# Two pieces of ScalarE work tied behind the kept product u3 in the second block of gates

## The chip, the cores and the metric

The kernel runs on one core of one Trainium2 chip. The metric is the device time of one execution in microseconds (us). A profiled execution gives the trace; other executions are timed without it.

## What is computed

For each of 8 batches and 8 heads of 64 features over 576 tokens:

```
kv  = k^T v                                (64 x 64 per head)
o   = q kv
x   = o / sqrt(mean(o*o) + 1e-6) * g_norm
```

The heads are laid side by side, so x is 4608 tokens by 512. Then

```
a = x w1;  b = x w2          (512 x 1024)
out = ((a * b) w3) w_out     (1024 x 1024, 1024 x 512)
```

q, k, v and g_norm are float32. The four weights arrive as float64 and are turned to float32 on the chip.

## The kernel before, in words

**Stages.** Weights come in chunks into four raw buffers. A chunk is *converted* from 64-bit words in steps (`conversion`, L137): ScalarE makes the low words (L158, into a part of `ab`) and the absolute value of the high words (L160, into the destination); VectorE then runs four passes (L162, L166, L169, L172); a chunk of w1 and w2 is scaled by g_norm at the end (L133 on ScalarE in the first group). There are 20 chunks. The first eight and some more are used at once, since w3 w_out is folded into one matrix `w3o_sb` at the start (`fold_chunk`, L681). The last four, chunks 2, 6, 3 and 7 of w1 and w2, are converted during the first group of gates. I call the last one w7.

**Groups.** The tokens are worked in nine groups of 512 (eight batches, and one of what is left of them). A group has four *blocks of gates* (p = 0 to 3) and then a projection. A block computes a part of a, b and a*b by Winograd's form of a two by two matrix product (`winograd`, L695): seven products on TensorE (L702), in three PSUM banks r1, r2, r3:

```
r1 = a11*b11, copied as p1;   r2 = s1*t1, copied as p5
r1 += s2*t2,  copied as u2;   (between)
r2 += s4*b22, c12;            r1 += s3*t3, copied as u3, c22
r3 = a12*b21, c11;            (between)
r1 += a22*t4, c21
```

The copies p1, p5, u2 and u3 are ScalarE's (`keep`, L713, copy at L715), each into a buffer of its name that exists once (u2 and u3 share one). A product that adds into a bank can't start before the copy of that bank has been taken. c11, c12 and c22 are VectorE's sums of a bank and a copy (L844) and a product (L845); c21 is a ScalarE copy (L839) and a VectorE product (L841).

**Work in the gaps.** At each `between` a piece of the attention of the next batch is issued (`steps`, L572; batch 1 during the first group). The first `between` of the second block (p = 1) issues the kv products of batch 1 (L334) and their six ScalarE copies (L342, L344). The second one issues `end_first`: q of batch 1, two tiles, was taken apart by ScalarE (L295), turned by a DMA transpose (L297), and is put together again by two ScalarE copies (L307). Behind each of them in SyncE's queue stands the load of the next q into the same tile (`load_q_ahead`, L472, at L95). The first `between` of the third block issues the product of q and kv (L412).

**What sets the order.** TensorE, GpSimd and SyncE run in the order of the program text (`manual_schedule`, L1288). ScalarE and VectorE are ordered by a planner when the kernel is built, from its own durations. `tc.issue_after(x)` ties the instructions in its block behind x where they are on x's engine. It adds no wait between engines. The conversions of the first group are begun at L1477 to L1484 after each block, two of them per block while there are some (n = 0, 1); the first two steps are tied behind a copy of that block, `ahead`. For p = 1 and n = 1 the chunk is w7; its VectorE passes and its scaling are issued at the first `between` of the third block (`between`, L1400). Its reader is the sum for the fourth block (`sum_w(3)`), issued after the third.

Of the kernel before, what the change touches and what calls it, by code (L numbers as in the profile page):

```python
# [22 lines left out]
def kernel(  # L23
# [64 lines left out]
    loaded, copies, adds = {}, {}, {}  # L88
# [164 lines left out]
    def all_of(steps):  # L253
        for _ in steps:
            pass
# [12 lines left out]
    xT = {B: x_left}  # L268
# [242 lines left out]
    def batch(b):  # L511
        if b not in batches:
            batches[b] = attention(b)
        return batches[b]
# [57 lines left out]
    def steps(b):  # L572

        a = batch(b)
        a.start()
        more = b + 1 < B
        fs, ends = ([[] for _ in range(8)] for _ in range(2))  # L580

        def turn(i, f, *args, next_group=False):

            t = []

            def begin():
                t.append(f(*args))
                next(t[0])
                next(t[0])

            fs[i].append((begin,))
            (to_end if next_group else ends[i + 1]).append((lambda: all_of(t[0]),))

        if to_end:

            ends[0] += [(lambda: nc.gpsimd.tensor_copy(tick, late["p5"][:, 0, 0:1]),), *to_end]
        to_end.clear()
        odd = b % 2
        by_scalar, in_two = b >= FIRST_OF_TWO, b > FIRST_OF_TWO
        if b == 1:  # L600
            early.extend(a.q_two_by_dma(r) for r in (0, 1))
            q_first = list(early)
            fs[0].append((a.begin_kv, 0))

            def end_first():
                for t in q_first:
                    with tc.issue_after(copies["kv"].ins):
                        next(t)
                    all_of(t)

            ends[1].append((end_first,))
        fs[2 if b == 1 else 1] += [(a.begin_kv, 1), (a.finish, 0)]
        if b == 1:
            last = {}

            def begin(name, behind, f, *args):
                last[name] = f(*args)
                with tc.issue_after(copies[behind][-1].ins):
                    next(last[name])
                next(last[name])  # L620

            def end(name, behind):
                with tc.issue_after(copies[behind][-1].ins):
                    next(last[name], None)
                all_of(last[name])

            fs[2] += [(begin, f"q{r}", "u2", a.q_two_by_dma, r) for r in (2, 3)]
            fs[3].append((begin, "left", "u3", a.q_left_by_dma))
            fs[4].append((begin, "x", "u3", a.x_by_dma, 0, nc.scalar.copy))
            ends[4] += [(end, "q2", "p1"), (end, "q3", "p5")]  # L630
            ends[5] += [(end, "x", "u2"), (end, "left", "u3")]
        elif by_scalar:
            turns_by_scalar(b)
        else:
            turn(1, a.q_two_by_dma, 2, 3)
            turn(2, a.x_by_dma, 0)
            if odd:
                turn(1, a.q_left_by_dma)
        second = 5 if b == 1 else 4
        if more:  # L640
            fs[6 if in_two else second].append((batch(b + 1).begin_kv, 0))
        fs[second].append((a.finish, 1))
        if odd:
            fs[3 if in_two else second + 1].append((a.product_left,))
        if b == 1:
            turn(6, a.x_by_dma, 1)
            turn(7, a.x_left_by_dma, next_group=True)
        else:
            if not by_scalar:
                turn(5, a.x_by_dma, 1)  # L650
            if odd:
                turn(5, a.x_left_by_dma, next_group=more)
        if more and not by_scalar:
            turn(7 if b == 1 else 5, batch(b + 1).q_two_by_dma, 0, 1, next_group=True)
        if more:
            fs[7 if odd else 0].append((load_q_left, b + 1))
        return iter([lambda s=e + f: [f(*args) for f, *args in s] for e, f in zip(ends, fs)])
# [101 lines left out]
    def run(*step_lists):  # L759

        for steps in zip(*step_lists):
            for step in steps:
                step()
# [52 lines left out]
    def sum_ab(p):  # L816
        aa[p] = {f"a{i + 1}{j + 1}": ab[j][:, p, i, :] for i in range(2) for j in range(2)}
        return sums(aa[p], free["ab", p])
# [300 lines left out]
    def sum_inner(n, between=lambda: None, place=None):  # L1119

        s1, s2, s4 = ab_sums
        x = [ab[0][:, :, 0], s1, s2, s4, ab[0][:, :, 1], ab[1][:, :, 0], ab[1][:, :, 1]][n]
        a11, a12, a21, a22 = (
            x[:, 2 * j:2 * j + 2, i * P:(i + 1) * P] for i in range(2) for j in range(2)
        )
        s1, s2, s4 = inner_sums[(n if place is None else place) % 3]
        nc.vector.tensor_add(s1, a21, a22)
        nc.vector.tensor_sub(s2, s1, a11)
        nc.vector.tensor_sub(s4, a12, s2)
        between()  # L1130
        nc.vector.tensor_sub(a21, a11, a21)
        inner[n] = [a11, a12, a22, s1, s2, s4, a21]
# [258 lines left out]
    for n, T in enumerate(groups):  # L1391
# [28 lines left out]
        if T in IN_TWO:  # L1420
            p = 2
# [15 lines left out]
        for p in range(NF):  # L1437
            if T in IN_TWO and p + 1 < NF:
                continue
            stage[0] = f"p{p}" if T in IN_TWO or T == FIRST_OF_TWO - 1 else None  # L1440
            if T and p + 1 == NF:
                sum_1, sum_2, sum_4, sum_3 = sum_ab(p)
                following = {
                    "c12": [], "c22": [sum_1],
                    "c11": [
                        lambda: sum_inner(0, lambda: all_of(f() for f in (sum_2, sum_3))),
                        lambda: sum_inner(1),
                    ],
                    "c21": [sum_4],
                }  # L1450

                if T in IN_TWO:
                    following["c22"].append(of_two[0])
                    following["c21"].append(of_two[1])
                if T not in TWICE:
                    in_order = tc.manual_schedule(engines={mybir.EngineType.DVE})
                    in_order.__enter__()
                gates(T, p, between, lambda name: all_of(f() for f in following[name]))
                continue
            gates(T, p, between if T or p else lambda: None)  # L1460
            if T == 0:

                def begin_early(behind):
                    t = early.pop(0)
                    with tc.issue_after(behind.ins):
                        next(t)
                    next(t)

                if p == 0:
                    begin_early(copies["xT"])  # L1470
                if p + 1 < NF:
                    ops = sum_w(p + 1)
                    if p != 2:
                        ops.pop(0)()
                    with tc.issue_after(adds["c12"][p].ins):
                        run(ops)
                for n in range(2):  # L1477
                    if len(converted) < len(todo):
                        ahead = [copies["p5"][p] if p else copies["xT"], copies["u2"][p]][n]
                        with tc.issue_after(ahead.ins):  # L1480
                            begin_next()
                        if len(begun) < len(todo):
                            with tc.issue_after(adds["c12"][0].ins):
                                end_next()  # L1484
                if p == 0:
                    begin_early(copies["u3"][0])
                if p + 1 == NF:
                    allocate_projection()
                    first, *others = zip(*(f(i) for i in range(NF) for f in (sum_ab, combine_w3o)))
                    with tc.issue_after(adds["c21"][p - 2].ins):  # L1490
                        all_of(step() for step in first)
                    with tc.issue_after(adds["c12"][p - 1].ins):
                        all_of(step() for steps in others for step in steps)
            else:
                ops = [step() for step in sum_ab(p)]
                with tc.issue_after(ops[-1].ins):
                    if p == 1:
                        prepare_some(3)
                    if (T, p) == (1, 1):
                        all_of(preparing)  # L1500
# [44 lines left out]
```

## Time and profile before

| | us |
|---|---|
| median of three runs | 751.8 |
| lowest and highest | 750.62, 752.29 |
| the profiled execution | 750.54 |
| its span in the trace | 748.7 |

In the trace's times, the first group's gates run from 84.1 us to about 140.7 and its projection to about 165. In the second block:

| ScalarE or TensorE work | start, us |
|---|---|
| p1, p5 | 97.96, 99.69 |
| u2 | 102.29 |
| low words of chunk 3 (L158) | 102.75 |
| absolute value of w7 (L160) | 103.83 |
| scaling of chunk 6 (L133) | 104.87 |
| kv copies | 105.91 to 107.23 |
| q copies (L307, two) | 107.13 to 109.36 |
| u3 | 109.38 |
| low words of w7 (L158) | 109.86 |
| TensorE, a22*t4 | 110.02 |
| c21 copy | 112.05 |
| p1 of the third block | 113.99 |

A time that a line gives as busy is from the first start to the last end of a run of equal instructions; neighbours on one engine overlap by about 0.1 us, so the spacing of starts is the cost of an instruction to its queue. "PE" is TensorE's matmuls, "PEld" its weight loads, "DVE" is VectorE, "ACT" ScalarE, "POOL" GpSimd, "SPq" SyncE's queue. The bracket at the end of a line holds the idle time of the engine before it, and what ended it.

### The profile page before, as it was taken

What the parts mean: (1) busy time and instruction counts of PE and PEld (TensorE: products, weight loads), DVE (VectorE), ACT (ScalarE), POOL (GpSimd) and SP (SyncE); (2) the same over time, 40 slices, a digit from 0 to 9 for tenths busy, and PEclk for the clock granted to TensorE, in tenths of its full rate; (3) what the DMA queues carried; (4) which work ended last, traced back from release to release, by engine and by line L of the source; (5) the groups of instructions that cost most, each with busy time, mean ns of one, the idle gap of its engine ahead of it and who ended that gap; (6) DMA issues with size and microseconds to landing.
All of it is one profiled execution on the core that took longest, in us unless ns stands there. A gap on an engine that the chain in (4) does not pass through costs nothing.

```text
span 748.7 us, 16771 instructions
## 1 busy us (share of the span) xinstructions
PE 740.2 (99%) x6759; PEld 659.3 (88%) x6759; DVE 640.2 (85%) x1339; ACT 361.3 (48%) x630; POOL 41.9 (6%) x46
## 2 busy tenths in 40 slices
PE   8999989999999999999999999999999999999998
PEld 6455778888899889999999999999999999999997
DVE  6977998747889877988898989898989997898897
ACT  6687777413321565347535763565367323222321
POOL 0000000133330100010000000100001000000000
PEclk9999999999999999999999999999999999999999
DMA  9996934438998996677967897689657663465354
GB/s 311 360 317 200 268 106 109 133 78 266 277 315 302 269 273 181 221 237 211 292 220 239 221 276 262 208 241 284 241 123 242 209 220 105 153 221 176 126 200 139
DMA packets 134737, 165.32 MB, mean 221 GB/s; under 512 B 77956, under 2 KB 110724, under 8 KB 134660
## 3 DMA queue, kind: packets, MB, share of 16 engines
q1 hardware_dynamic: 132208, 149.84, 66.0%
q10 hardware_dynamic: 2452, 14.42, 5.7%
q8 instruction: 53, 0.87, 0.5%
q14 instruction: 24, 0.20, 0.1%
HBM read 126.22 MB, written 20.71 MB: 196 GB/s over the span
## 4 chain that ended last, share of the span: by engine, by line
PE 95%; ACT 2%; DVE 1%; DMA 1%; issue 1%; SPq 0%; ACTq 0%
PE mm L702 42%; PE mm L1169 23%; PE mm L960 18%; PE mm L681 6%; PE at L334 2%; PE at L412 1%; PE mm L412 1%; PE at L668 1%; DMA raw<-in_moe_w_out_dram 1%; PE at L1220 0%; ACT ab L158 0%; DVE ab L162 0%; PE at L431 0%; ACT chunks L160 0%; ACT w_sb L160 0%
## 5 line engine op out<-in xcount | busy, mean ns | idle before, releaser
L702 PE MATMUL mm<-xT,w_sb 128*128 128x256 f32 x528 | 121.2, 380 | 0.0
L702 PEld LDWEIGHTS mm<-xT,w_sb 128*128 128x128 f32 x528 | 99.7, 191 | 13.3 <-issue 0.5
L702 PE MATMUL mm<-xc,ws 128*128 128x256 f32 x384 | 87.0, 380 | 0.0
L702 PEld LDWEIGHTS mm<-xc,ws 128*128 128x128 f32 x384 | 73.0, 190 | 10.1 <-ACT p L715 0.4
L681 PE MATMUL mm<-chunks,ab 128*128 128x512 f32 x128 | 60.4, 604 | 0.9 <-DVE chunks L172 0.9
L715 ACT COPY u<-mm 128x512 f32<-128x512 f32 x42 | 24.6, 585 | 59.8 <-PE mm L702 43.5
L715 ACT COPY p<-mm 128x512 f32<-128x512 f32 x50 | 29.4, 588 | 46.9 <-PE mm L702 30.6
L1180 ACT COPY u<-mm 128x512 f32<-128x512 f32 x23 | 13.5, 586 | 77.3 <-DVE raw L1193 39.8
L1169 PE MATMUL mm<-w3o_sb,ab 128*128 128x128 f32 x368 | 48.6, 276 | 0.0
L702 PE MATMUL mm<-xc,w_sb 128*128 128x256 f32 x192 | 46.4, 385 | 2.1 <-ACT u L715 2.1
L1169 PE MATMUL mm<-w3o_sb,raw 128*128 128x128 f32 x372 | 48.1, 276 | 0.0
L960 PE MATMUL mm<-ws,w3o_sb 128*128 128x128 f32 x300 | 46.3, 276 | 0.0
L1169 PEld LDWEIGHTS mm<-w3o_sb,ab 128*128 128x128 f32 x368 | 45.4, 192 | 0.4
L1169 PEld LDWEIGHTS mm<-w3o_sb,raw 128*128 128x128 f32 x372 | 44.8, 192 | 0.0
L702 PEld LDWEIGHTS mm<-xc,w_sb 128*128 128x128 f32 x192 | 35.7, 190 | 7.6 <-ACT u L715 2.7
L681 PEld LDWEIGHTS mm<-chunks,ab 128*128 128x128 f32 x128 | 21.8, 190 | 23.4 <-issue 15.3
L702 PE MATMUL mm<-xT,ws 128*128 128x256 f32 x176 | 42.3, 384 | 0.0
L380 DVE TENSOR_REDUCE inv<-sq 128x8 f32<-128x512 f32 (+1 forms) x40 | 24.3, 628 | 20.8 <-ACT sq L379 20.8
L960 PEld LDWEIGHTS mm<-ws,w3o_sb 128*128 128x128 f32 x300 | 39.8, 192 | 0.0
L702 PEld LDWEIGHTS mm<-xT,ws 128*128 128x128 f32 x176 | 32.9, 190 | 4.6
L839 ACT COPY c<-mm 128x256 f32<-128x256 f32 x24 | 8.9, 371 | 57.8 <-PE mm L702 57.8
L845 DVE TENSOR_TENSOR ab<-c 128x256 f32<-128x256 f32 x72 | 34.9, 484 | 1.9
(244 smaller groups left out, 1686.2 us busy)
## 6 DMA issues: line engine op xcount, KB each, us to landing
w3o_sb<-w3o_l SPq DMA_DIRECT2D x18, 896.0 KB, 6.6
w3o_sb<-w_l SPq DMA_DIRECT2D x18, 896.0 KB, 5.9
raw<-in_moe_w_dram SPq DMA_DIRECT2D x31, 512.0 KB, 7.7
raw<-w3o_l SPq DMA_DIRECT2D x15, 896.0 KB, 4.7
w3o_sb<-w3o_l ACTq DMA_DIRECT2D x14, 896.0 KB, 5.1
k_sb<-in_k_dram SPq DMA_DIRECT2D x16, 576.0 KB, 4.9
v_sb<-in_v_dram SPq DMA_DIRECT2D x16, 576.0 KB, 6.6
q_sb<-in_q_dram SPq DMA_DIRECT2D x32, 256.0 KB, 3.7
```

The costliest lines, as they stand in the source:

```text
L334: nc.tensor.matmul(ps[r * D:(r + 1) * D, :], lhsT=k_sb[rows, r, cols], rhs=v_sb[rows, r, cols], start=(j == 0), stop=(j == JS - 1),)
L380: adds["norm"] = nc.vector.tensor_reduce(out=inv[:, i], in_=sq.rearrange("p (h d) -> p h d", d=D), axis=AX.X, op=ALU.add)
L412: nc.tensor.matmul(o_ps[l][tokens, n * D:(n + 1) * D], lhsT=qT[r][rows, e, i, tokens], rhs=kv_b[rows, m // 2 ^ l, e, h, :], start=True, st ...
L668: nc.tensor.transpose(t_ps[:, m, :], src, ident)
L681: nc.tensor.matmul(sums_ps[half][m], lhsT=w3T[half, c][:, m, :], rhs=chunks[:, c, 1, :], start=(c == 0), stop=(c == KF - 1),)
L702: nc.tensor.matmul(ps[:, u, :], lhsT=lhsT(a_name, u, c), rhs=rhs(b_name, c),  start=(u == 0 and c == 0 and to is None), stop=(c == chunks ...
L715: copies.setdefault(name, []).append(nc.scalar.copy(t, ps))
L839: copied = nc.scalar.copy(c, one[:, 0, :])
L845: nc.vector.tensor_mul(dst, c[:, 0, :], c[:, 1, :])
L960: nc.tensor.matmul(ps[place // 4][:, place % 4, :], lhsT=x, rhs=y, start=new and place // 4 not in seen, stop=True, skip_group_check=True,)
L1169: nc.tensor.matmul(to[:, i, :], lhsT=x[:, c, :], rhs=y[:, c, :], start=new and place // 4 not in seen, stop=(c == 1), skip_group_check=True,)
L1180: nc.scalar.copy(t[:, 0:4], ps[0])
```

## The change

Two ties are moved to the copy u3 of the second block. In `end_first` the two q copies were tied behind the last kv copy; they are tied behind u3. (The `between` that calls it comes after u3 in the program text, so the last u3 in the list is that of the second block.) Where the conversions are begun, the first two ScalarE steps of the chunk with p = 1 and n = 1, w7, were tied behind u2 of that block; they are tied behind its u3. Nothing is added or left out, and SyncE's order stays.

```
             def end_first():
                 for t in q_first:
-                    with tc.issue_after(copies["kv"].ins):
+                    with tc.issue_after(copies["u3"][-1].ins):
                         next(t)
                     all_of(t)
...
                 for n in range(2):
                     if len(converted) < len(todo):
-                        ahead = [copies["p5"][p] if p else copies["xT"], copies["u2"][p]][n]
+                        ahead = [copies["p5"][p] if p else copies["xT"], copies["u3" if p == 1 else "u2"][p]][n]
                         with tc.issue_after(ahead.ins):
                             begin_next()
```

More of the change, by code (lines that the diff above doesn't have):

```diff
@@ L606, in end_first @@
                 for t in q_first:
-                    with tc.issue_after(copies["kv"].ins):
+                    with tc.issue_after(copies["u3"][-1].ins):
                         next(t)
@@ L1478 @@
                     if len(converted) < len(todo):
-                        ahead = [copies["p5"][p] if p else copies["xT"], copies["u2"][p]][n]
+                        ahead = [copies["p5"][p] if p else copies["xT"], copies["u3" if p == 1 else "u2"][p]][n]
                         with tc.issue_after(ahead.ins):
```

## The prediction

> **What bounds the kernel now.** I read the page's busy shares first, then TensorE's waits over the whole span, then the chain that ended last around the one wait that is left, then the timeline there.
>
> ```profile
> PE 740.2 (99%) x6759; PEld 659.3 (88%) x6759; DVE 640.2 (85%) x1339; ACT 361.3 (48%) x630; POOL 41.9 (6%) x46
> PE 95%; ACT 2%; DVE 1%; DMA 1%; issue 1%; SPq 0%; ACTq 0%
> ```
>
> TensorE is busy for 740.2 of 748.7 us and is 95% of the chain. Any time that another engine gives back counts only where TensorE stands still, so the list of its waits is the list of what can be won (columns: waiter, releaser, us in total, times, longest):
>
> ```profile
> PE mm L702 <- ACT u L715: 2.1, 1, 2.1
> PE mm L274 <- POOL ident masks.py:199: 1.4, 1, 1.4
> PE mm L681 <- DVE chunks L172: 0.9, 1, 0.9
> PE at L668 <- DVE chunks L172: 0.8, 1, 0.8
> ```
>
> The lower three lie in the start-up. The first is a single wait for a kept product's copy (L715), and it is the place of the change. The chain in that place (start, us, what):
>
> ```profile
> 103.94 1.05 ACT w_sb L160
> 104.99 1.04 ACT w_sb L133
> ...
> 107.23 2.14 ACT qT L307 x2
> 109.38 0.59 ACT u L715
> 109.97 0.04 issue
> 110.02 7.17 PE mm L702 x32
> ```
>
> The same stretch in the timeline of all engines:
>
> ```profile
> 104.35 3.62 PE L702 MATMUL mm<-xT,w_sb 128*128 128x256 f32 x16
> 105.47 0.69 DVE L166 TENSOR_SCALAR w_sb<-w_sb 128x1024 f32<-128x1024 f32 x1
> 107.13 2.23 ACT L307 COPY qT<-q_sb 128x1024 uint16<-128x1024 uint16 x2
> 108.32 1.44 SPq L95 DMA_DIRECT2D q_sb<-in_q_dram  x2
> 109.86 1.16 ACT L158 ACTIVATE ab<-raw 128x1024 f32<-128x1024 uint32 x1
> 110.02 2.00 PE L702 MATMUL mm<-xc,w_sb 128*128 128x256 f32 x8 [2.06 <-ACT u L715]
> 112.08 1.22 DVE L162 SCALAR_TENSOR_TENSOR ab<-raw,ab 128x1024 uint32<-128x1024 uint32 x1
> ```
>
> One product of a block is 8 TensorE instructions, 1.73 us (16 take 3.46 from start to start). The 16 at 104.35 are s3*t3 into bank r1, done at about 106.08, and a12*b21. The next product, a22*t4, writes r1 again, so it needs the copy u3 of r1. ScalarE could start u3 at 106.1. It starts at 109.38, because the kv copies and the two q copies stand ahead of it. a12*b21 is done at 107.96 (110.02 less 2.06): TensorE stands 2.06 us.
>
> [...] u3's input is complete at 106.1, and it runs 3.3 us later behind the q copies. [...] The trace has 0.586 (L715) and 1.05 between starts; I use the trace's.
>
> **The change, part by part.** Both edits leave the instructions as they are and tie some to a later place on ScalarE.
>
> *The q copies (two of L307).* They leave the place before u3: 2.25 us between the starts at 107.13 and 109.38. They run right after it instead. Their own readers are far: the product that reads qT (L412) is at 118.2, 8.8 us after they end at 109.36. Nothing is bought there as long as they end by about 116. With each pair come the loads of the next q (L95, SyncE's queue, 108.32), which wait until q_sb has been read. SyncE's order is fixed and the next entry is the k/v load at 118.49; the loads' readers are the copies at 120.02 and 122.05. With u3 first, the copies end between about 109.0 and 109.5, as before, so the loads move by no more than a few tenths: cost 0. GpSimd has nothing in this stretch.
>
> *The first steps of the last weight chunk (w7, L158 and L160).* In the trace of before, only the Abs pass (L160, 103.83) is ahead of u3; the low-word pass (L158, 109.86) is already behind it. So this takes 1.05 us from before u3. The Abs pass feeds VectorE's L166 at 105.47 (0.60 us between starts), which now comes later too. The chunk's reader is the sum for the fourth block at 125.76, and its four VectorE passes end at 116.6 and its scaling by g at 118.9: 6.8 us of cover.
>
> *When u3 runs after.* Left before it are: u2 and the low words of the chunk before (to 103.94), the scaling L133 of w6, which needs VectorE's L172 of 103.19 to 104.41, and the kv copies (1.22 us, their products are done at 102.6). In the slower order: L133 104.45 to 105.5, kv to 106.7, u3 106.7 to 107.3. In the faster one u3 starts at 106.2. TensorE needs it at 107.96: covered by 0.6 us or more. The wait of 2.06 us goes.
>
> *What is late next.* TensorE arrives 2.06 us earlier at the third block. There the product s2*t2 writes r1 again and needs the copy p1. It stood at 113.99 to 114.57, TensorE wanted it at 115.31 (113.58 plus 1.73); now TensorE wants it at 113.25. ScalarE from the slower u3: free at 107.2; q copies to 109.45; L158 and L160 to 111.55; the c21 copy 0.27; the scaling L133 of the chunk before, 1.05, to 112.87; p1 to 113.45. That is 0.2 late. The other input of that copy is its buffer, free after VectorE's c11 add (113.21 to 113.9 in before). VectorE runs without a gap here except the 0.51 us that it waited for u3; with L166 still ahead of the add it ends near 113.2 and p1 near 113.85: 0.6 late; with L166 and L162 of w7 behind the add it ends near 111.6 and costs nothing. Bounds 0 (a gain is excluded, since no other wait on this path remains) and 0.85 (both queues in their slower order, with 0.25 for semaphores and starts, an estimate from the gaps in the chain). I take **0.35**.
>
> *The rest of the third block.* u3 there is copied 123.70 to 124.28 against TensorE's 124.55: 0.27 us of slack. It hangs on a ScalarE run without a gap from 117.28, which starts from TensorE's own s2*t2 and so moves with it; the scaling of w7 in that run needs VectorE's last pass, and that one comes forward by the 0.51 us gap and the passes' order. I give it 0 beyond the 0.35. Further on, the turn of x on GpSimd ends near 153.5 and group 1 starts at about 165.5: 10 us of cover. After that TensorE has no wait in the list, so what is won is kept to the end.
>
> **Sum.** −2.06 + 0.35 = **−1.7 us**. The profiled execution took 750.54 (span 748.7), which becomes 748.8. It lies 1.3 below the median of the runs, 751.8, so the median becomes **750.1**. The case's own range is a gain of 1.2 to 2.06: 749.7 to 750.6.
>
> **Rivals.** *The gain is given back in the third block.* The place is the same p1 copy and the u3 with 0.27 us of slack behind it. For it: ScalarE has only about 2 us idle between 110 and 117.3 (1.03+0.52+0.93 less what the copies need), and 3.3 us are pushed there; VectorE has none. Against it: w7 is not needed until 125.76 and can stand aside. Loss 0.85 at p1 and 0.6 at u3 instead of 0.35: gain 0.6, time 751.2. Chance 0.25.
>
> *Slower: the four VectorE passes of w7 slip past the third block's start.* The order of VectorE and ScalarE is chosen by the planner when the kernel is built, from its own durations. Between 118.3 and 121.7 VectorE is idle (3.40 us), so passes that start by 118 are hidden; if the planner sets them between the reduces (L380, 121.71) and the c12 add (122.91), that add waits for 1.13+0.60+0.60+1.13 = 3.46 us, the third u3 copy waits for the add, and TensorE stands 3.46−0.27 = 3.2. With 1.7 won before: 751.8−1.7+3.2 = 753.3. It decides from about 2 us of passes at that place on. Against it: their ScalarE inputs are ready at 111.6, 10 us earlier. Chance 0.10.
>
> *The change does not do what it says*: the planner puts other ready ScalarE work ahead of u3, or the kv copies later. By the trace, the other work up to there (p1, c21 and the scaling of the chunk before) has no input yet. Time 751.8, chance 0.05.
>
> **How the numbers follow.** A measurement of this kernel can tell about 0.2% (1.5 us) from no change; the three runs shown lie 1.7 us apart. My case has 0.60: its middle passes 1.5 us but its lower end does not, so 0.51 faster, 0.09 same. The second gives 0.03 faster, 0.20 same, 0.02 slower; the slower one 0.07 slower, 0.03 same; the last 0.05 same. Sums: faster 0.54, same 0.37, slower 0.09. The range: the full 2.06 and 0.9 of scatter below, 748.8; above, no gain at all with a little scatter, 752.0. It leaves out most of the slower case.
>
> **What would show it.** Right: TensorE's list of waits has no "ACT u L715" of 2.1 us; u3 starts at 106.2 to 106.8 with the q copies after it; a22*t4 starts near 108.0 instead of 110.02; any new wait is on the p1 copy near 113.3 and under 0.85 us; the fourth block's first product (126.3 in before: 124.55 plus 1.73) comes 1.7 earlier. Wrong: u3 still behind a copy of 1 us or more; a wait of over 1 us in the third or fourth block for u3 or a VectorE sum; the SyncE loads of q later than 112.

## The result, and the profile after

The median after is **749.03 us** (seven executions, 748.15 to 749.29) against 751.8 before (seven, 750.5 to 752.29): ratio 0.9965, 95% interval 0.9954 to 0.9977, or 2.6 us faster (1.7 to 3.5). The forecast was 750.1 in a range of 748.8 to 752.0. The profiled execution after took 749.29, with a span of 747.5: only 1.25 less than the profiled one before. The result therefore sets two questions: why the profile shows less than was forecast, and why the timed executions show more than the profile.

First the top of TensorE's list of waits after (waiter, releaser, us in total, times, longest; three lines of 0.7 us and less that follow are left out, none of them in the first group's gates):

```profile
PE mm L274 <- POOL ident masks.py:199: 1.4, 1, 1.4
PE at L668 <- DVE chunks L172: 0.8, 1, 0.8
PE mm L702 <- ACT u L715: 0.7, 1, 0.7
```

The wait for u3 went from 2.1 to 0.7 us, not to nothing. The chain after, in the same place, says what holds the rest:

```profile
103.16 1.22 DVE w_sb L172
104.38 1.15 DVE ab L162
105.52 0.02 issue
105.55 1.23 DVE w_sb L172
106.77 0.60 DVE c L844
107.37 0.61 DVE ws L755
107.98 0.59 ACT u L715
```

Before, this chain ran over ScalarE (w7's absolute value, a scaling, kv, q). Now it runs over VectorE. The timeline of ScalarE, VectorE and TensorE there:

```profile
104.32 3.62 PE L702 MATMUL mm<-xT,w_sb 128*128 128x256 f32 x16
105.55 1.23 DVE L172 CUSTOM_DVE_ANT_0 w_sb<-w_sb,ab 128x2048 uint16<-128x2048 uint16 x1
106.69 0.68 DVE L844 TENSOR_TENSOR c<-mm,u 128x512 f32<-128x512 f32 x1
106.81 1.15 ACT L133 ACTIVATE w_sb<-w_sb,g_col 128x1024 f32<-128x1024 f32 x1 [0.57 <-DVE w_sb L172]
107.98 0.59 ACT L715 COPY u<-mm 128x512 f32<-128x512 f32 x1
108.46 2.23 ACT L307 COPY qT<-q_sb 128x1024 uint16<-128x1024 uint16 x2
108.62 1.99 PE L702 MATMUL mm<-xc,w_sb 128*128 128x256 f32 x8 [0.69 <-ACT u L715]
112.97 0.59 ACT L715 COPY p<-mm 128x512 f32<-128x512 f32 x1
```

The q copies and w7's steps are behind u3, as the change says. But the planner has filled the opened place: the scaling (L133) of chunk 3, the one before w7, now stands ahead of u3. In the kernel before it came at 112.32, behind c21. It waits 0.57 us for VectorE's last pass of chunk 3 (L172), which the planner has pulled from 110.61 to 105.55, ahead of the c12 sum. VectorE before, for comparison:

```profile
106.07 0.68 DVE L844 TENSOR_TENSOR c<-mm,u 128x512 f32<-128x512 f32 x1
110.61 1.22 DVE L172 CUSTOM_DVE_ANT_0 w_sb<-w_sb,ab 128x2048 uint16<-128x2048 uint16 x1
```

The place that L172 took on VectorE had been w7's L166 (105.47 in before), which came later because its input, the absolute value of w7, now stands behind u3. So the change opened a place on two engines, and both were filled. (u3 starts at 107.98, where the scaling ends, 106.81 plus 1.15. That the chain names VectorE's L755 for the last 0.6 us is its inference from what ended last before; no data goes from that sum to u3.) Outside the second block and the start of the third the two instruction orders are the same, and within them only those of ScalarE and VectorE differ.

The wait fell by 2.06−0.69 = 1.37 us. At a22*t4 of the third block TensorE is 1.25 ahead (123.30 against 124.55); the 0.1 between went into a short wait for that block's u3. At the end the span is 1.2 shorter. So the profiled pair is explained by this one wait.

### The profile page after: what moved, and what is told of

Same layout as the page of the kernel before. It is cut to its first block, busy times and chain, and to the rows that moved or that the text cites. A ratio compares the mean times of both kernels' runs of the same rounds, so it can differ in the third digit from the quotient of the medians.

```text
span 747.5 us, 16773 instructions
## 1 busy us (share of the span) xinstructions
PE 740.4 (99%) x6759; PEld 658.8 (88%) x6759; DVE 639.6 (86%) x1339; ACT 361.8 (48%) x630; POOL 40.9 (5%) x46
## 4 chain that ended last, share of the span: by engine, by line
PE 92%; DMA 3%; DVE 3%; ACT 1%; issue 0%; SPq 0%; ACTq 0%; DVEq 0%
PE mm L702 40%; PE mm L1169 22%; PE mm L960 18%; PE mm L681 5%; PE at L334 2%; DMA raw<-in_moe_w_dram 2%; PE at L412 1%; DMA raw<-in_moe_w_out_dram 1%; PE mm L412 1%; DMA w3o_sb<-w3o_l 1%; PE at L668 1%; DVE ab L162 1%; DVE w_sb L172 0%; PE at L1220 0%; ACT ab L158 0%
## 5 line engine op out<-in xcount | busy, mean ns | idle before, releaser
L845 DVE TENSOR_TENSOR ab<-c 128x256 f32<-128x256 f32 x72 | 32.5, 452 | 1.9
```

Of the source, the lines that this page charges most:

```text
L845: nc.vector.tensor_mul(dst, c[:, 0, :], c[:, 1, :])
```

## The experiments

Each kernel was timed beside the kernel before. *Full clock* means that the mean granted TensorE clock of an execution was listed as 0.999 or 1.000; the reason for that split is in the first run.

**e1, the kernel before again.** No edit.

> The kernel before, unchanged, once more: a control. All theories: ratio 1 within its interval (0.998 to 1.002). What it tells apart is whether the first profile was typical. Theory A (one wait, the same in every execution): TensorE's list has one wait for ACT u L715 of 2.0 to 2.1 us again. Theory C (the gain of the timed runs, 2.6 us, has a part that the first profile of before does not show): the wait is 2.5 us or longer, or other waits appear.

Ratio 0.9992 (0.9982 to 1.0002). The wait is 2.1 us as before, so the first profile's wait was typical. But the execution profiled took 751.8 us, 1.3 more than the first one, and had a mean clock of 0.997. Busy time by stretch (length, then PE, PEld, DVE, ACT and POOL), with the granted clock third from the end:

```profile
108.00:110.00 2.00, 0.23 (x1) 0.23 (x2) 1.49 (x4) 1.98 (x4) 0.00 (x0) 1.00 0.42 86
110.00:112.00 2.00, 2.00 (x8) 1.67 (x8) 2.00 (x4) 0.78 (x1) 0.00 (x0) 0.73 0.59 185
112.00:114.00 2.00, 2.00 (x7) 1.55 (x6) 2.00 (x4) 1.42 (x2) 0.00 (x0) 0.50 0.00 0
114.00:116.00 2.00, 2.00 (x10) 1.75 (x9) 2.00 (x4) 0.59 (x1) 0.00 (x0) 0.92 0.00 0
```

Right behind TensorE's wait (108 to 109.8) the clock falls to half and is back within 116. Lost: 2 x (0.27+0.50+0.08) = 1.7 us. In the first profile of before the clock is 1.00 in all four stretches, after the same wait. Of this kernel's 14 executions, 7 had full clock (749.67 to 750.5, median 749.8) and 7 had 0.997 or 0.998 (751.43 to 753.01, median 751.7). So the times of before are two groups; their medians lie 1.9 us apart here and 1.6 to 1.9 in the executions of before timed beside the later runs, where the groups overlap at the edges. By its signs theory A came true (one wait, 2.1 us) and theory C did not (no longer wait, no further one). What C supposed is there all the same: a part of the timed gain that the first profile of before does not show, in the form of a slower clock behind the wait.

**e2, the q copies alone; e3, w7 alone.** Each takes one line of the change's diff.

> Only the q copies are tied behind u3; the first steps of w7 stay tied to u2. Theory A (the time is TensorE's wait for u3 and nothing else, and any ScalarE work that the planner finds ready is put in the opened place): the built order has both steps of w7 ahead of u3 (about 1.05 us each), so u3 starts near 108.3 and the wait is 0.8 to 1.1 us; 0.9 to 1.2 us faster than before. Theory B (the q copies alone are the matter and the tie of w7 does nothing): no wait is left, as much faster as the change or more, 2 us or over.

> Only the first steps of w7 are tied behind u3; the q copies stay behind the kv copies. Theory A: u3 starts 1.05 us sooner than before less what fills the place, near 108.4, wait of about 1.1 us, 0.8 to 1.1 us faster than before. Theory B: nothing is won, the wait stays at 2 us, within 0.2 us of before.

e2: ratio 0.998 (0.997 to 0.9991), wait 0.95 us. e3: ratio 0.998 (0.9971 to 0.999), wait 1.1 us, and 0.2 more for u3 of the third block. By the waits theory A holds in both and theory B falls. By time alone e2 can't be told from the whole change: its median at full clock is 749.0, that of the change 749.03 and 749.07. ScalarE in e2:

```profile
103.78 1.15 ACT L160 ACTIVATE w_sb<-raw 128x1024 f32<-128x1024 f32 x1
107.07 1.15 ACT L158 ACTIVATE ab<-raw 128x1024 f32<-128x1024 uint32 x1
108.25 0.59 ACT L715 COPY u<-mm 128x512 f32<-128x512 f32 x1
```

Without w7's tie the planner draws its low words (L158), which had been behind u3 in before, ahead of it into the place of the q copies. In e3 the q copies are ahead (105.67), and u3 is at 107.92. Each half wins about 1 us of the wait for u3, both together 1.37: the halves don't add, since in each something else steps into the place.

**e4, the rest of chunk 3 behind too.** On the changed kernel, where the two conversions are begun:

```
-                            with tc.issue_after(adds["c12"][0].ins):
-                                end_next()
+                            with tc.issue_after(adds["c12"][p].ins):
+                                with tc.issue_after(copies["u3"][p].ins):
+                                    end_next()
```

> The change, and besides the rest of the conversion of the chunk before w7 (its VectorE passes behind the c12 sum of the second block, its scaling on ScalarE behind u3). Theory A: in the changed kernel u3 was held by that scaling, which was put ahead of it and waited for VectorE's L172, and by the c12 sum. With both behind, u3 starts by 106.3 and TensorE has no wait there: 0.6 to 0.8 us faster than the changed kernel, 2.0 us faster than before. Rival (given back in the third block): u3 is early but p1 of the third block is late, TensorE waits 0.3 us or more there, and the time is that of the changed kernel within 0.3 us.

Ratio 1.0002 (0.9992 to 1.0012): all the gain gone. In the second block it works, u3 starts at 106.36 and TensorE has no wait. The third block pays (ScalarE, then TensorE):

```profile
118.24 1.15 ACT L133 ACTIVATE w_sb<-w_sb,g_col 128x1024 f32<-128x1024 f32 x1 [2.04 <-DVE w_sb L172]
124.81 3.68 PE L702 MATMUL mm<-xc,w_sb 128*128 128x256 f32 x8 [2.44 <-ACT u L715]
```

Chunk 3's passes now lie close ahead of w7's in VectorE's queue, so w7's last pass ends at 118.2 instead of 116.7 in the changed kernel. ScalarE's scaling of w7 waits for it, and behind that scaling in its queue stand the kv copies, a q copy and the squares, which the reduces, c12 and so the third u3 need. A wait of 2.1 was traded for one of 2.4, in a place that was not touched. The rival had put its 0.3 us or more at p1 of the third block; the loss came at u3 of that block and was eight times that. (e7 below tests this account: it moves that one scaling, and the wait is gone.) Half of the executions (7 of 14) had a lower clock here too, and in the profile the dip (0.74, 0.50, 0.91) comes behind the wait in the third block, at 124 to 130, not at 110.

**e5, the changed kernel again; e6, the wait of before filled.** e6 puts this ahead of a22*t4 of the second block of the kernel before:

```
+            t = bank(ps_at, "at")
+            for _ in range(8):
+                nc.tensor.matmul(t[:, 0:P], lhsT=ident, rhs=ident, start=True, stop=True)
```

> The changed kernel once more, a control on the chip of the next three. All theories: 0.996 to 0.998 of before. Clock theory (where TensorE stands some 2 us, the chip in some executions grants it less clock for a few us after, 1.7 us in the one profile of before that has it; a wait of 0.7 us is too short for that): the wait is 0.7 us, the clock in the stretch 100 to 130 is 1.00, and the runs lie closer together than those of before. Rival (the scatter of before has nothing to do with the wait): the runs scatter as much as before's.

> The kernel before with eight dummy products of the unit matrix into a spare PSUM bank set ahead of a22*t4 of the second block: some 1.8 us of useless TensorE work in the place of the wait, nothing else moved. Clock theory: TensorE does not stand, so no clock is lost after it; profile within 0.3 us of the first profile of before (750.5), median 0.6 to 1.2 us below before, runs within about 1 us. Rival (before's upper runs come from elsewhere): same median as before within 0.3 us and the same scatter. If the dummy products end later than u3 they cost 0.1 to 0.3 us.

e5: ratio 0.9976 (0.9968 to 0.9984), wait 0.7 us, all 22 executions at full clock. e6: ratio 0.9994 (0.9983 to 1.0005); median 750.19, 0.4 below before, less than the 0.6 to 1.2 expected, and the ratio alone is inconclusive. The clocks are not: 13 of 14 executions had full clock. TensorE in e6, the useless products and then the product that waits:

```profile
107.81 1.95 PE L737 MATMUL at<-ident 128*128 128x128 f32 x16
110.03 1.99 PE L702 MATMUL mm<-xc,w_sb 128*128 128x256 f32 x8 [0.27 <-ACT u L715]
```

a22*t4 starts at 110.03, as in before. The full-clock median is 750.15, that of before timed beside it 750.34. So with TensorE kept busy, the wait still costs its 2 us, and the lower clock is nearly gone. Its one low execution (753.75) and some upper ones at full clock (751.16, 751.68) have another cause, which no run here settles.

**e7 and e10, all of it moved.** On e4, the scaling of w7 alone goes behind u3 of the third block; its VectorE passes keep their place in the program. The first line is in `conversion`, ahead of its scaling, the rest in `between`:

```
+        yield
...
             if len(converted) < len(begun):
-                with tc.issue_after(copies["u2"][-1].ins):
-                    end_next()
+                if len(copies["u3"]) > p:
+                    with tc.issue_after(copies["u3"][-1].ins):
+                        end_next()
+                else:
+                    for c in begun[-1]:
+                        next(c)
```

> The change, the rest of the chunk before w7 behind c12 and u3 as in the fourth run, and the scaling of w7 on ScalarE behind u3 of the third block, which in the fourth run was what came late. My theory: u3 of the second block starts by 106.4, TensorE has no wait there, and the third block's u3 no longer waits for the scaling of w7: no wait for ACT u L715 above 0.3 us, 0.6 us faster than the changed kernel in the profile (span 746.8 to 747.0) and 2.0 us faster than before plus what the clock cost before. Rival: the work shows up in a third place, the sum for the fourth block or its p copies, with a wait of 0.5 us or more, and nothing is won over the changed kernel.

> The kernel of the seventh run once more, for its interval: 0.996 to 0.9975 of before, no wait for u3, no execution with a mean clock under 0.9985.

Ratios 0.9961 (0.9947 to 0.9975) and 0.9949 (0.9936 to 0.9962), medians 748.11 and 747.95: **the best version**, about 1 us below the changed kernel. All 11 executions had full clock. TensorE's waits in e10 are all in the start-up (this kernel's lines are one higher):

```profile
PE mm L275 <- POOL ident masks.py:199: 1.4, 1, 1.4
PE at L669 <- DVE chunks L172: 1.1, 2, 0.8
PE mm L682 <- DVE chunks L172: 0.3, 1, 0.3
PE at L335 <- ACT qT L357: 0.2, 1, 0.2
```

**e8 and e11, u3 held longer.** On the changed kernel, u3 of the second block is copied three times (e8) or five times (e11, with 4 for the 2) instead of once, the same copy to the same place:

```
+            if name == "u3" and len(copies.get("u3", [])) == 1:
+                for _ in range(2):
+                    nc.scalar.copy(t, ps)
```

> The changed kernel with u3 of the second block copied three times, the first two for nothing: ScalarE is held 2 x 0.48 to 2 x 0.59 us longer ahead of a22*t4. One to one (TensorE's wait goes whole into the time): wait 1.65 to 1.9 us and 1.0 to 1.2 us slower than the changed kernel. Rival (later slack takes a part back): under 0.6 us slower. Clock theory: at this length some executions may lose clock too, up to 1.7 us more in those.

> The changed kernel with u3 of the second block copied five times, four of them for nothing. One to one: wait 2.9 to 3.2 us, and the executions at full clock 2.2 to 2.5 us slower than the changed kernel's (749.05), 751.2 to 751.6. Clock theory: a longer wait takes the clock in more of the executions than the half or less of before (2.1 us) and of the run with two more copies (1.9 us): over 6 in 10, each 1.5 to 2 us slower again. Rival: the part with a lower clock is about the same as before, so that the length of the wait is not what decides.

e8: wait 1.9 us, ratio 0.9998 (0.9988 to 1.0007). Its full-clock median is 749.9, 0.8 above that of the changed kernel (749.07): under the 1.0 to 1.2 expected, and two thirds of the 1.2 us of added wait. 5 of 14 executions had a lower clock. e11: wait 3.2 us, ratio 1.003 (1.0017 to 1.0043). Full clock in 3 of 20 only, at 751.05 (2.0 above, for 2.5 us of added wait); the 17 others have a median of 753.2. The profile of e11, clock third from the end:

```profile
108.00:112.00 4.00, 1.39 (x4) 1.16 (x5) 2.91 (x6) 3.87 (x7) 0.00 (x0) 0.89 0.02 4
112.00:114.00 2.00, 2.00 (x6) 1.59 (x5) 1.22 (x3) 1.71 (x3) 0.00 (x0) 0.50 0.47 129
```

So a longer wait loses the clock more often, and the rival (the same part as before) falls.

**e9, only the scaling of chunk 3 moved.** On the changed kernel:

```
                             with tc.issue_after(adds["c12"][0].ins):
-                                end_next()
+                                with tc.issue_after(copies["u3"][p].ins):
+                                    end_next()
```

> The change, and of the chunk before w7 only the scaling on ScalarE behind u3 (its VectorE passes stay where the planner put them, ahead of c12). The step of my prediction on what is late next: u3 starts near 107.45, when c12 has read u2, so the wait for u3 falls from 0.7 to 0.1 us, but q copies, scaling and both steps of w7 are then ahead of p1 of the third block, which ends near 114.0 against TensorE's 113.3: a wait of 0.3 to 0.9 us for ACT p L715 and the time of the changed kernel within 0.3 us. Rival: no wait for p1, 0.6 us faster than the changed kernel.

Ratio 0.997 (0.9959 to 0.9982), median 749.31, the same as the changed kernel. Two lines of ScalarE and one of TensorE:

```profile
107.15 0.58 ACT L715 COPY u<-mm 128x512 f32<-128x512 f32 x1 [1.25 <-DVE c L844]
113.17 1.07 ACT L715 COPY p<-mm 128x512 f32<-128x512 f32 x2
113.81 1.99 PE L702 MATMUL mm<-xc,ws 128*128 128x256 f32 x8 [0.57 <-ACT p L715]
```

With the scaling away, u3 stands idle for 1.25 us until c12 has read u2: the two copies share one buffer. The wait for u3 is 0.2, and 0.57 comes back at p1 of the third block, as the prediction's step on what is late next had it.

**The clock, over all runs.** TensorE's longest wait in the gates, and the executions that had a mean clock of 0.998 or less (one execution of 1092 us left out):

| kernel | longest wait, us | lower clock | median at full clock, us |
|---|---|---|---|
| e7, e10, all moved | none | 0 of 11 | 748.1, 748.0 |
| e6, wait filled | 0.3 | 1 of 14 | 750.15 |
| e9 | 0.6 | 0 of 8 | 749.3 |
| the change, e5 | 0.7 | 0 of 29 | 749.03, 749.07 |
| e2 | 1.0 | 1 of 22 | 749.0 |
| e3 | 1.1 | 0 of 12 | 749.8 |
| e8 | 1.9 | 5 of 14 | 749.9 |
| before, e1 | 2.1 | 54 of 131 | 749.8 to 750.4 |
| e4 | 2.4 | 7 of 14 | 750.3 |
| e11 | 3.2 | 17 of 20 | 751.05 |

From a wait of 0.7 to one of 3.2 us the part with a lower clock grows; among 1.9, 2.1 and 2.4 these numbers show no difference. Only profiled executions show where the clock was lost: in e1, e4 and e11 it was right behind the wait. That it was so in the others is argued from their mean clock. One loss of 1.7 us in 750 gives 0.9977, which fits the 0.997 and 0.998 of most of them; 0.995, as in e2's one low execution (755.57 us) and five of e11, would take two. The profile of e2 has no wait above 0.95 us in the gates, so the cause of that execution is open.

**Where the clock fell in the profiled executions.** The waits, beside the granted clock of the stretches at their end and behind them (from and to, us):

| profile | wait, us | granted clock behind it | lost, us |
|---|---|---|---|
| e11 | 3.17 | 108 to 112: 0.89; 112 to 116: 0.50, 0.88 | 1.7 |
| e4 | 2.44 | 124 to 130: 0.74, 0.50, 0.91 | 1.7 |
| e1 | 2.07 | 110 to 116: 0.73, 0.50, 0.92 | 1.7 |
| before | 2.06 | 110 to 116: 1.00 | none |
| e8 | 1.9 | 110 to 116: 1.00 | none |
| e3, e2, the change | 1.11, 0.95, 0.69 | 110 to 116: 1.00 | none |

The products behind the wait show the same loss: the 8 of a22*t4 and the 8 that follow took 2.69 and 2.92 us in e1 (109.77 and 112.25) against 2.00 and 1.89 in before (110.02 and 111.85), 1.7 us more together. The same wait of 2.06 or 2.07 us thus cost the clock in e1 and not in the first profile of before. What sets two executions of one kernel apart in this, these runs do not show.

## Why the prediction was right, and what was wrong in it

The direction and the place were right, and 749.03 lies in the range of 748.8 to 752.0, near its lower end; the range of the case itself, 749.7 to 750.6, was missed. The term of 1.7 us stood for 2.6 (1.7 to 3.5) measured. That the two are near each other is in part luck, two errors of opposite sign: at full clock the change gives 1.25, and the rest is the clock, which the sum did not have. The first result also had more of the slower executions of before (five of seven, by their times) than the longer series (54 of 131). e5, with 22 executions against 43, gives 1.8 us (1.2 to 2.4), of which 1.27 at full clock.

*What bounds.* Right: the list of TensorE's waits held what can be won at full clock. In every run but e6, which keeps the wait and fills it, the full-clock median, against that of before timed beside it, moved with the sum of the waits for u3 and p1, to within 0.5 us.

*"The wait of 2.06 us goes."* **Wrong by 0.69**, the step that failed. It has two parts. First, "u3 runs from 106.2 to 106.7": u3 can't start before c12 has read u2 from the buffer that they share; my start was taken from s3*t3 alone. e9 shows that wait by itself (1.25 us for DVE c L844). In the VectorE order of before, c12 ended at 106.75, and in the order after at 107.37, so this part alone would cost little: 0.20 us in e9, where the scaling is moved away. Second, and for most of the 0.69, "the other work up to there has no input yet", by which I gave the planner's filling a chance of 0.05. The prediction saw that w7's L166 would come later on VectorE, but not that another pass would take its place. The planner moved chunk 3's VectorE pass 5 us forward and c12 0.6 back, and so gave the scaling of chunk 3 an input. e2 shows the same in another form (low words drawn forward). That the change frees a place on an engine whose order is planned had to be read as: the place will be filled, from whatever is ready by the planner's durations.

*"p1 of the third block is late: 0.35."* Measured 0 in the changed kernel: p1 ended at 113.56, TensorE wanted it at 113.91. The scaling of chunk 3 was no longer between u3 and p1, as it was ahead of u3; and TensorE came 0.7 us later than reckoned (113.25), since that much of the wait for u3 was left. The price was right where the premises held: in e9 the scaling is behind u3, only 0.20 us of the wait for u3 is left, and TensorE waits 0.57 us at p1, inside my 0 to 0.85.

*"The rest of the third block: 0."* About 0.1 us was lost at its u3, whose slack of 0.27 was used up.

*The q loads.* They moved by 1.3 us (109.66), not by "a few tenths", since u3 came later than forecast; TensorE had no wait behind them. Two side sums are off without bearing on the result: ScalarE's idle time between 110 and 117.3 leaves out the 1.20 us before u2 of the third block, and the cover from 153.5 to 165.5 is 12 us, not 10.

*The slower rival*, work slipping ahead of the third block's c12, did not come with the change, but e4 brought a loss at the place it names: 2.44 us of wait for u3 of the third block. The way there was another. No pass stood between the reduces and c12; w7's last pass only ended 1.5 us later and had started at 116.99, which by the prediction's reckoning ("passes that start by 118 are hidden") costs nothing. It held up the scaling on ScalarE, and with it the squares that the reduces need. I had thought of VectorE's queue alone.

*What the sum lacked.* The wait of 2.1 us costs 2.1 us of standing and, by the mean clock, in 54 of 131 executions of before some 1.6 to 1.9 us more (1.7 in the one that was profiled, e1, where the granted clock behind the wait was down to 0.50). The profile of before that I had was one at full clock, 1.3 us below its median, and I carried that difference along as scatter instead of asking for its cause. The seven executions of before behind the first result fall in two groups as well (750.5 and 750.62, five from 751.68 to 752.29), and the seven after all have full clock. That their difference of 2.77 is 1.25 plus a part of the 1.9 fits this, but it is argued, since the clocks of those seven weren't recorded.

## What to carry to other kernels

Moving work away from in front of a critical instruction on an engine whose order is planned frees a place, and the planner fills it; compare the two built orders, and tie the next candidates as well, following each tied piece to the queue that it lands in (e4 lost everything, e7 won 1 us more by one further tie). Ask of a late copy what holds its target buffer, not only its source. And price a wait of TensorE of some 2 us at more than its length, here 1.7 us more in the one profile of before that shows a loss, with a lower mean clock in 54 of 131 executions of before: look at the granted clock of several executions before one profile is taken as the time.

## What the runs showed of the hardware that was not expected

A wait of TensorE was followed by a lower granted clock in some executions and not in others of the same kernel. After 2.07 us (e1) the clock was 0.73, 0.50 and 0.92 in the three stretches of 2 us from 110 us on, and 1.7 us were lost; after 2.06 us (the first profile of before) and 1.9 us (e8) it was 1.00 in all three. The part of the executions with a lower mean clock was 1 of 71 for waits of 0.6 to 1.1 us (e9, the change, e2, e3), 5 of 14 for 1.9, 54 of 131 for 2.1, 7 of 14 for 2.4 (e4) and 17 of 20 for 3.2. Filling the wait with useless products (e6) left 1 of 14. Why one execution lost its clock and the next did not, and what brought it down in the single executions of e2 and e6, these runs don't show.
